# Hedgehog attention and a spatial gating unit on one core: another order of the same work

## The chip, the cores and the metric

The kernel runs on one core of a Trainium2 chip. A core has five engines that each work through their own queue of instructions: PE (TensorE, matrix products), DVE (VectorE), ACT (ScalarE), POOL (GpSimd) and SP (SyncE, which here only issues transfers). The metric is the time of one launch on the device in microseconds, the median over several runs.

## The reference

Two stages follow each other. The first is linear attention with a softmax-like feature map: every query and key vector of 64 numbers is projected to 128, the largest absolute value is taken off, and exponentials of both signs give 256 features. The second is a gated MLP whose gate mixes the 576 positions of a sequence.

```python
def phi(x):                                   # x is q or k: 8 batches, 8 heads, 576 positions, 64
    proj = einsum('bhsd,df->bhsf', x, w_phi)  # 128 features
    proj = proj - max(abs(proj), axis=-1, keepdims=True)
    return concatenate([exp(proj), exp(-proj)], axis=-1)
...
kv  = einsum('bhsf,bhsd->bhfd', k_p, v);  z = sum(k_p, axis=2)
num = einsum('bhsf,bhfd->bhsd', q_p, kv)
den = einsum('bhsf,bhf->bhs', q_p, z)[..., None] + 1e-06
x   = num / den                               # reshaped to 8 batches, 576 positions, 512
...
h = maximum(x @ w_in, 0.0)                    # 1024 wide
u, v = h[..., :512], h[..., 512:]
v_n = (v - mean(v)) / sqrt(var(v) + 1e-06)
v_s = einsum('ts,bsd->btd', w_spatial, v_n) + b_spatial[None, :, None]
out = (u * v_s) @ w_out
```

## The kernel before

Each batch of 576 positions is cut into 512, which are four chunks of 128, and a tail of 64. Two batches share one tail tile of 128 rows, and four such pairs are worked beside the eight batches. All products are in bfloat16, all sums in eight banks of 2 KB per partition.

The code has no loop over batches. Every step is a small function marked `@op`, and a string, `ORDER`, lists some 1,400 words, each of which calls one step. A word reads `name.arguments:places@engine`: `tkc.0.1.0@V` is the copy of transposed keys of batch 0 on VectorE (A is ScalarE, P GpSimd, S SyncE), and the places are the banks or the numbered buffers that it writes. The last lines of the kernel walk through the string. No scheduler changes the order: each engine gets its instructions as the words stand, and a wait holds back all that is queued behind it on that engine.

The steps of one batch, with the lines at which the profile shows them:

- `lk`, `lq` load keys and queries by GpSimd's transfer queue (lines 358 and 362), `lv`, `lkt` and others on SyncE's. For batch 0 the keys come in four quarters as 32-bit numbers (`lkf`), and `ckf` casts each (line 257). `lin`, `lout`, `lsp` load weights by GpSimd's queue.
- `tk`, `tq` transpose on TensorE (line 488), `tkc`, `tqc` copy the result into T (line 257 on VectorE, line 255 on ScalarE).
- `kp`, `qp` project (line 540). `km`, `qm` reduce to the largest absolute value into mk and mq: on VectorE, line 545.
- `ke` and `qe` take the exponentials on ScalarE (lines 549 and 675). For keys the factor of the maximum goes into the values: `kem`/`kee` (line 554), then `vs` on GpSimd (line 605; for tails `vst`, line 620). `kv` multiplies (lines 640 and 642), `kvc` copies.
- For queries the maximum is split (`qs`, lines 657 and 658), transposed (`qt`, line 662), copied into mT (`qc`), and taken off as a second product into the same bank (`qf`, lines 666 and 670).
- `qn` multiplies with kv (line 724), `qr` and `qx` divide (lines 730 and 737). `tx` transposes x, `txc` copies.
- `vm` and `um` are the two halves of the first layer (lines 839 and 937); `vr` and `ur` evict with a relu (line 261 on ScalarE, 263 on VectorE). `vb`, `va`, `vx`, `vy` are the statistics (lines 867, 873, 844 and 847), `vw` the root on GpSimd (line 850), `vn` the normalised values (line 853).
- `sm` mixes the positions (lines 952 and 954), `sg` gates (line 961), `om` is the last layer (line 966), `oc` copies it, `od` stores it.
- A further `t` in a name (`vrt`, `vnt`, `omt`) is the same step for a pair of tails.
- `omh`, `och`, `odh` do one tile of the last batch in two halves of 256 columns (lines 985 and 997), so that the last store is small.
- `warm` and `warmh` are fillers: matmuls of 512 or 256 columns (lines 334 and 342) on zeros, whose result no one reads.
- `cident`, `csel`, `csel2`, `cphi`, `zvnt`, `chalf` make constants; `spt`, `spc`, `spb` transpose the spatial weights into w_spT and put the bias row behind them. `spb` is four small casts on GpSimd.

Numbers behind a name count batch, chunk or half: `km.4.0` reduces the first quarter of the keys of batch 4.

Of the kernel before, what the change touches and what calls it, by code (L numbers as in the profile page):

```python
# [17 lines left out]
zsp@V lq0.4.4:0 zvst.0@V lq0.0.4 cident@P csel@V csel2@V lkf.0:0@A lkf.1:1@S lphi@A lkf.3:2@S zvnt.0@V ckf.0:1@V  # L18
lkt.0:0@S ckf.1@P cphi@V warm.10:0 tk.0.0.0:0 tk.0.0.1:1 zmhl.0@V tkc.0.0.0:0@V tkc.0.0.1@A warm.3:2 kp.0.0:2,3
kp.0.1:4,5 ke.0.0.0:0 lkf.2:3@S km.0.1:0 warm.4:6 tq.0.1.1:0 tqc.0.1.1:1@V tq.0.1.0:1 ke.0.0.1 lv.0.0:0@S tqc.0.1.0@V  # L20
ckf.3@P tk.0.1.1:6 tkc.0.1.1:2@A km.0.0 lqt.0:1@S kem.0.1:0 vsz.0.1:0@P ke.0.1.0:1 chalf@P warm.4:7 kp.0.3:0,1
km.0.3:1 zmhl.2@V lq.1:2 ckf.2@V ke.0.1.1 warm.3:7 tq.0.0.0:2 tq.0.0.1:3 qp.0.0.1:6,7 tqc.0.0.1:3@V ckt.0:0@P
warmh.2:2 tkt.0:4 lk.1:0 tqc.0.0.0@A ke.0.3.0:2 lin.0 tk.0.1.0:5 tktc.0:0@V tkc.0.1.0@V qp.0.0.0:2,3 vs.0.1.1@P
warm.1:4 kp.0.2:4,5 lq.2:1 lin.1 ke.0.3.1 qm.0.0.1:0 ke.0.2.0:3 qm.0.0.0 kpt.0:0,1 qp.0.1.0:6,7 qm.0.1.0:1 qs.0.0:0@P
qp.0.1.1:2,3 warm.1:6 qt.0.0:6 ket.0.0:0 vs.0.1.0@P kem.0.0 qm.0.1.1 ket.0.1 qc.0.0:0@A kmt.0:2 cqt.0:0@V warm.2:7
qf.0.0.0:6,7 ke.0.2.1 qf.0.0.1:2,3 km.0.2 warm.4:0 tq.1.0.1:0 tqc.1.0.1:4@V tqt.0:1 tqtc.0:0@V qs.0.1:2@P vsz.0.0:1@P
qt.0.1:4 qc.0.1:1@V qe.0.0.0.1:0 vs.0.0.0@P lvt.0:0@S tq.1.1.1:5 kemt.0:1 qe.0.0.0.0 tq.1.0.0:6 qe.0.0.1.0:1
tq.1.1.0:7 qpt.0:0,1 tqc.1.0.0@V tqc.1.1.1:5@V kem.0.2:2 vs.0.0.1@P qmt.0:2 vstz.0:0@P warm.2:4 qf.0.1.1:4,5
qe.0.0.1.1 qp.1.1.0:2,3 qm.1.1.0:3 lv.0.1:1@S vst.0.0.0@P vsz.0.2:2@P tqc.1.1.0@A vst.0.0.1@P kv.0.1:6 qp.1.0.1:0,1
qe.0.1.1.1:2 kv.0.0:7 qm.1.0.1:0 qe.0.1.1.0 kem.0.3 qp.1.1.1:2,3 qm.1.1.1 kvc.0.0:0@A qst.0:0@P kvc.0.1@A qf.0.1.0:4,5  # L30
lkt.1:0@S vs.0.2.1@P vs.0.2.0@P lbs:0@S tk.1.0.0:7 tk.1.0.1:0 qtt.0:1 qct.0:2@V qe.0.1.0.1:3 tkc.1.0.1:6@V qe.0.1.0.0
# [116 lines left out]
            qf=5, rc=3, x=3, xt=1, xT=3, xTt=2, vr=5, st=4, mv=6, rs=5, vn=3, vnt=2, uT=3, uTt=2, ob=5)  # L148
# [933 lines left out]
```

## Time and profile before

| what | us |
|---|---|
| median of 3 runs | 257.66 |
| lowest and highest | 256.53, 257.89 |
| profiled execution | 256.3 |
| its span, first instruction to last | 254.2 |
| TensorE busy | 244.1 (96%) |
| VectorE busy | 222.3 (87%) |
| ScalarE busy | 192.0 (76%) |
| GpSimd busy | 156.2 (61%) |

A row of instructions reads: line, engine, operation, what it writes and reads, shape and count, then busy time. The chain of waits is followed back from the last instruction: at each step to what released it, or to the instruction before it on its engine. A row of it gives start, length and what it was. A row of busy time by stretch gives for each engine the time and the count of instructions begun. PE's pieces overlap, since a matmul starts while the one ahead drains.

### The profile page before, as it was taken

To read this page: it belongs to the slowest core of one execution; us is meant where nothing else is said; L and a number is where in the kernel's file an instruction comes from. 1 tells how busy PE (TensorE), PEld (TensorE's weight loads), DVE (VectorE), ACT (ScalarE), POOL (GpSimd) and SP (SyncE) were. 2 spreads that over 40 slices of the span, in tenths; PEclk is the share of its full clock that TensorE was granted. 3 is DMA by queue.
4 is the path that set the end of the run, shared out by engine and by line. 5 is a ranking of instruction groups with operands and counts; after the bars stand their busy time and mean duration, and the time that the engine had idled before them with its cause. 6 is when DMAs were issued, how large, how long until landed. Compare 5 with 4: busy or idle time off the path is not lost.

```text
span 254.2 us, 8049 instructions
## 1 busy us (share of the span) xinstructions
PE 244.1 (96%) x3298; PEld 150.0 (59%) x3298; DVE 222.3 (87%) x417; ACT 192.0 (76%) x300; POOL 156.2 (61%) x244
## 2 busy tenths in 40 slices
PE   6968999999999999999999999999999999999994
PEld 2646865876546675756575555566566664545542
DVE  6899999999999999999999999899778883966472
ACT  2799999999999989969998986879997821122321
POOL 5399998829695879799879263675394130085000
PEclk9999999999999999999999999999999999999999
DMA  7999999899999499759989999194424606004265
GB/s 177 262 217 210 208 213 207 149 289 225 151 167 201 74 237 187 191 73 185 127 185 188 210 307 212 25 229 143 125 85 44 85 9 160 0 3 165 83 200 213
DMA packets 77911, 40.79 MB, mean 160 GB/s; under 512 B 46770, under 2 KB 73266, under 8 KB 77876
## 3 DMA queue, kind: packets, MB, share of 16 engines
q1 hardware_dynamic: 59956, 29.77, 54.3%
q0 software_dynamic: 17424, 10.10, 29.7%
q8 instruction: 25, 0.41, 0.7%
q10 hardware_dynamic: 496, 0.43, 0.5%
q14 instruction: 10, 0.08, 0.1%
HBM read 32.82 MB, written 9.44 MB: 166 GB/s over the span
## 4 chain that ended last, share of the span: by engine, by line
PE 63%; DVE 21%; POOL 7%; issue 6%; ACT 1%; DVEq 0%; POOLq 0%; ACTq 0%
PE banks L952 10%; PE banks L966 9%; PE banks L839 9%; PE banks L937 7%; DVE mk L545 6%; PE banks L640 5%; DVE mq L545 5%; PE banks L724 4%; PE banks L540 4%; POOL vs L605 3%; PE banks L954 2%; PE banks L666 2%; PE banks L670 2%; PE banks L1032 1%; DVE x L737 1%
## 5 line engine op out<-in xcount | busy, mean ns | idle before, releaser
L675 ACT ACTIVATE qf<-banks 128x1024 bf16<-128x1024 f32 x72 | 70.4, 1037 | 8.8 <-PE banks L670 6.4
L605 POOL TENSOR_TENSOR vs<-v,em 128x512 bf16<-128x512 f32 x62 | 64.0, 1048 | 6.3 <-ACT em L554 4.7
L549 ACT ACTIVATE kf<-banks 128x1024 bf16<-128x1024 f32 x64 | 63.0, 1038 | 3.1 <-PE banks L540 1.9
L545 DVE TENSOR_REDUCE mk<-banks 128x8 f32<-128x1024 f32 x36 | 43.3, 1212 | 0.8 <-PE banks L540 0.7
L545 DVE TENSOR_REDUCE mq<-banks 128x8 f32<-128x1024 f32 x36 | 43.1, 1216 | 0.6 <-PE banks L540 0.2
L850 POOL TENSOR_TENSOR rs<-mv,neghalf 128x4 f32<-128x4 f32 (+2 forms) x13 | 11.1, 855 | 45.0 <-DVE mv L844 44.8
L952 PE MATMUL banks<-w_spT,vn 128*128 128x512 bf16 x128 | 32.9, 379 | 0.1
L839 PE MATMUL banks<-w_v,xT 128*128 128x512 bf16 x128 | 32.6, 379 | 0.1
L937 PE MATMUL banks<-xT,w_u 128*128 128x512 bf16 x128 | 32.4, 379 | 0.1
L966 PE MATMUL banks<-w_out,uT 128*128 128x512 bf16 x124 | 30.7, 379 | 0.0
L255 ACT COPY ob<-banks 128x512 f32<-128x512 f32 (+1 forms) x21 | 12.3, 592 | 22.1 <-PE banks L966 21.7
L961 DVE TENSOR_TENSOR uT<-banks,uT 128x512 bf16<-128x512 f32 x32 | 21.4, 684 | 4.7 <-PE banks L954 3.9
L867 DVE BATCH_NORM_STATS2 st<-vr 128x6 f32<-128x512 bf16 x32 | 21.5, 678 | 4.0 <-ACT vr L261 3.9
L640 PE MATMUL banks<-vs,kf 128*128 128x66 bf16 x512 | 23.9, 194 | 0.1
L640 PEld LDWEIGHTS <-kf 128*128 128x128 bf16 x512 | 21.6, 97 | 3.7 <-issue 0.2
L540 PE MATMUL banks<-wphi,T 64*128 64x128 bf16 x512 | 22.8, 217 | 0.9 <-DVE mq L545 0.3
L261 ACT ACTIVATE vr<-banks 128x512 bf16<-128x512 f32 (+1 forms) x22 | 13.3, 611 | 12.3 <-POOL vn L853 5.9
L737 DVE TENSOR_TENSOR x<-banks,rc 128x512 bf16<-128x512 f32 x32 | 21.8, 686 | 0.8 <-DVE rc L730 0.2
L853 POOL TENSOR_SCALAR vn<-vr,mv,rs 128x512 bf16<-128x512 bf16 x27 | 20.4, 764 | 2.5 <-DVE mv L847 1.8
L724 PEld LDWEIGHTS <-qf 128*128 128x128 bf16 x512 | 19.1, 97 | 3.8 <-ACT qf L675 0.2
L642 PE MATMUL banks<-vst,kft 128*128 128x66 bf16 x128 | 21.1, 192 | 0.0
L540 PEld LDWEIGHTS <-T 64*128 64x128 bf16 x512 | 15.6, 94 | 8.9 <-issue 6.3
(122 smaller groups left out, 454.3 us busy)
## 6 DMA issues: line engine op xcount, KB each, us to landing
v<-in_v_dram SPq DMA_DIRECT2D x16, 512.0 KB, 9.2
out_dram<-ob SPq DMA_DIRECT2D x31, 256.0 KB, 2.6
ld<-in_q_dram POOLq DMA_DIRECT2D x7, 512.0 KB, 9.9
ld<-in_k_dram POOLq DMA_DIRECT2D x7, 512.0 KB, 9.0
out_dram<-ob SPq DMA_DIRECT2D x9, 128.0 KB, 2.5
tf<-in_k_dram SPq DMA_DIRECT2D x8, 128.0 KB, 7.4
tf<-in_q_dram SPq DMA_DIRECT2D x8, 128.0 KB, 7.8
vt<-in_v_dram SPq DMA_DIRECT2D x8, 128.0 KB, 5.2
```

The lines of the kernel that those rows point to most:

```text
L540: nc.tensor.matmul(out=bank(banks[y])[:, n * F:(n + 1) * F], lhsT=xT[halves[y], n, :], rhs=wphi[halves[y], :], start=True, stop=True)
L545: nc.vector.tensor_reduce(out=out_, in_=pp.rearrange("p y (n f) -> p y n f", f=F), axis=AX.X, op=ALU.max, apply_absolute_value=True)
L549: nc.scalar.activation(out=kf[:, s].rearrange("p y n f -> p y (n f)"), in_=pp, func=AF.Exp, bias=0.0, scale=(1.0, -1.0)[s])
L605: ENG[e].tensor_tensor(out=at["vs", (b, j)][:, s, :, 0:D], in0=at["v", (b, j // 2)][:, (j % 2) * n:(j % 2 + 1) * n, :], in1=at["em", (b, j ...
L640: nc.tensor.matmul(out=pv[:, hh, s, :], lhsT=kf[:, s, c % 2, 2 * hh + c // 2, :], rhs=w[:, s, NB * hh + c, :], start=(c == 0), stop=False)
L675: nc.scalar.activation(out=at["qf", u][:, s].rearrange("p y n t -> p y (n t)"), in_=at["pq", u], func=AF.Exp, bias=0.0, scale=(1.0, -1.0)[s])
L724: nc.tensor.matmul(out=at["pn", u][:, y, n, :], lhsT=f[:, s, y, n, :], rhs=at["kv", b][:, hg * HH + n, s, :], start=(s == 0), stop=(s == 1))
L737: nc.vector.tensor_tensor(out=at["x", (b, cc)][:, :, hg * HH:(hg + 1) * HH, :], in0=at["pn", u][:, :, :, 0:D], in1=at["rc", u].to_broadcas ...
L839: nc.tensor.matmul(out=bank(place)[r], lhsT=lhs[:, kc, r], rhs=w_v[:, kc, :], start=(kc == 0), stop=(kc == KC - 1))
L937: nc.tensor.matmul(out=bank(place).rearrange("p (c t) -> p c t", c=NB), lhsT=w_u[:, kc, dc * P:(dc + 1) * P], rhs=at["xT", b][:, :, kc, :] ...
L952: nc.tensor.matmul(out=bank(place), lhsT=at["vn", b][:, c, cs], rhs=w_spT[:, c, 0:T0], start=(c == 0), stop=False)
L966: nc.tensor.matmul(out=bank(place), lhsT=at["uT", b][:, dc, c * P:(c + 1) * P], rhs=w_out[:, dc, :], start=(dc == 0), stop=(dc == KC - 1))
```

## The change

Only the string `ORDER` is another one. The functions, the buffers and their numbers stay. Nearly every line of the string differs; what differs in substance:

- Fillers: 40 of 512 columns where there were 34, and the two of 256 columns (`warmh.2`) are gone. All stand in the first part of the table, ahead of batch 1's first layer.
- Engines of copies, with their number: `qc` five from ScalarE to VectorE and two back, `tkc` three from ScalarE to VectorE; `ur` six and three, `vr` six and four, `oc` five and eight (to ScalarE the second of each); `ckf.1` goes from GpSimd to VectorE, `ckf.2` from VectorE to GpSimd, two `vs` of batch 7 from VectorE to GpSimd.
- The order at the start, `spb` on GpSimd, loads on SyncE's and GpSimd's queues, and the order of the last tiles; the tile that is stored in halves is (7,2) instead of (7,1).

The last words of the table:

```diff
-om.7.3:2 oc.7.3:0@V od.5.3@S od.7.3@S om.7.0:3 om.7.2:0 oc.7.0:4@V od.7.0@S oc.7.2:2@A od.7.2@S omh.7.1.0:1
-omh.7.1.1:0 och.7.1.0:1@A odh.7.1.0@S och.7.1.1:3@V odh.7.1.1@A
+od.7.3@S od.7.1@S om.5.3:6 oc.5.3:2@A od.5.3@S omh.7.2.0:7 omh.7.2.1:0 och.7.2.0:1@A odh.7.2.0@S och.7.2.1:3@V
+odh.7.2.1@A
```

In the old words the second half output `omh.7.1.1` writes bank 0, which `om.7.2` wrote two products earlier. In the new ones `omh.7.2.1` writes bank 0, and the products ahead of it (`om.5.0:6 om.7.0:7 om.7.3:4 om.7.1:5 om.5.3:6`) use others.

VectorE's queue at the start of the program, before. `sel` is a constant for the queries' maxima, `vnt` a buffer that is preset, `ld` the keys, `T` their transposed copy:

```order
L301 TENSOR_TENSOR sel_169<-ident 128x16
L303 TENSOR_TENSOR sel_169<-sel_169 128x8
L307 TENSOR_SCALAR sel<-sel_169 128x1024
L257 COPY vnt_153<-ident 128x512 x2
L257 CAST ld_63<-ob_160 128x512
L257 CAST wphi<-wphi_f 64x128 x2
L316 MEMSET mhl_107 128x64
L257 COPY T_65<-banks 128x512
L545 TENSOR_REDUCE mk_87<-banks 128x2x4
```

The same place after the change:

```order
L301 TENSOR_TENSOR sel_169<-ident 128x16
L303 TENSOR_TENSOR sel_169<-sel_169 128x8
L257 COPY vnt_153<-ident 128x512 x2
L257 CAST ld_62<-ob_161 128x512
L257 CAST ld_62<-ob_160 128x512
L257 CAST wphi<-wphi_f 64x128 x2
L307 TENSOR_SCALAR sel<-sel_169 128x1024
L257 COPY T_65<-banks 128x512 x2
L316 MEMSET mhl_109 128x64
L545 TENSOR_REDUCE mk_87<-banks 128x2x4
```

A second cast of keys stands ahead of the first copy and the first reduction, `sel` is behind the weights' casts, and both copies of the first keys come ahead of the reduction.

GpSimd's queue between the values of batch 1 (`vs`) and the first normalised values of batch 0 (`vn`), before:

```order
L358 DMA ld_62<-in_k_dram 128x8x256
L422 DMA vn_150<-in_moe_w_spatial_dram 128x2304
L257 CAST w_spT<-uT_155 1x512
L257 CAST w_spT<-uT_155 1x64
L257 CAST w_spT<-uT_155 1x512
L257 CAST w_spT<-uT_155 1x64
L605 TENSOR_TENSOR vs_95<-v_74,em_94 128x8x64 x2
```

And after the change, where the four casts stand again:

```order
L605 TENSOR_TENSOR vs_98<-v_75,em_91 128x8x64 x2
L850 TENSOR_TENSOR rs_145<-mv_140,neghalf 128x4
L257 CAST w_spT<-uT_155 1x512
L257 CAST w_spT<-uT_155 1x64
L257 CAST w_spT<-uT_155 1x512
L257 CAST w_spT<-uT_155 1x64
L853 TENSOR_SCALAR vn_151<-vr_134,mv_140,rs_145 128x512
L853 TENSOR_SCALAR vn_151<-vr_130,mv_140,rs_145 128x512
L257 CAST tl_76<-tf_78 128x512
L362 DMA ld_64<-in_q_dram 128x8x256
```

`spb` has moved from ahead of batch 1's `vs` to between the root of batch 0 (`vw.0.2`) and the first `vn`, and two loads that stood ahead of that root now come behind.

ScalarE's last instructions, before:

```order
L261 ACTIVATE uT_2_157<-banks_61 128x512
L255 COPY ob_3_163<-banks_61 128x512
L255 COPY ob_2_162<-banks_61 128x512
L255 COPY ob_1_161<-banks_61 128x256
L997 DMA out_0_dram<-ob_3_163 128x256
```

And after the change:

```order
L255 COPY ob_3_163<-banks_61 128x512
L255 COPY ob_4_164<-banks_61 128x512
L255 COPY ob_0_160<-banks_61 128x512
L255 COPY ob_2_162<-banks_61 128x512
L255 COPY ob_1_161<-banks_61 128x256
L997 DMA out_0_dram<-ob_3_163 128x256
```

Four full output copies in a row now stand on ScalarE ahead of the half one, where there were two.

More of the change, by code (lines that the diff above doesn't have):

```diff
@@ L17 @@
 ORDER = """
[L18 to L31, printed above, removed]
-kv.0.2:6 tkc.1.0.0@A vs.0.3.0:3@P qn.0.0.0:2,3 qft.0:0,1 kvc.0.2@V qr.0.0.0:0 qx.0.0.0:0 qet.0.0:4 vsz.0.3@P
```

233 lines of the change are left out of this document (124 added, 109 removed).

## The prediction

> **What bounds the kernel now.** I read the page's totals and its chain first, then busy time by stretch, then the long pieces of the chain in order of time, and last the start, the middle and the tail piece by piece.
>
> ```profile
> span 254.2 us, 8049 instructions
> PE 244.1 (96%) x3298; PEld 150.0 (59%) x3298; DVE 222.3 (87%) x417; ACT 192.0 (76%) x300; POOL 156.2 (61%) x244
> ...
> PE 63%; DVE 21%; POOL 7%; issue 6%; ACT 1%; DVEq 0%; POOLq 0%; ACTq 0%
> ```
>
> TensorE holds 63% of the chain and VectorE (DVE) 21%. An average hides where each rules, so next the busy time of every engine by stretch:
>
> ```profile
> core 0: us, PE busy (x) PEld busy (x) DVE busy (x) ACT busy (x) POOL busy (x), PEclk, DMA share, GB/s
> ...
> 12.00:20.00 8.00, 5.64 (x88) 3.60 (x87) 7.91 (x12) 7.57 (x13) 7.54 (x13) 1.00 1.30 213
> ...
> 50.00:75.00 25.00, 24.93 (x313) 15.28 (x310) 24.49 (x48) 24.16 (x38) 16.76 (x29) 1.00 1.35 216
> 75.00:100.00 25.00, 24.43 (x416) 16.59 (x416) 24.71 (x47) 23.36 (x35) 18.85 (x30) 1.00 0.99 170
> ...
> 220.00:245.00 25.00, 25.00 (x152) 11.91 (x150) 16.73 (x36) 6.06 (x11) 9.33 (x12) 1.00 0.31 106
> ```
>
> From 12 us to 100 us VectorE is busy almost without a hole (7.91 of 8.00; 24.71 of 25.00). TensorE seems as full after 50 us, but pipelined matmuls overlap in that column, so a short stall doesn't show there. At 220 us only TensorE is full (VectorE 16.73 of 25.00). So there are two regimes. First VectorE's back-to-back queue sets when TensorE may go on; later TensorE's own work does. The chain shows the border:
>
> ```profile
> 6.20 0.62 PE banks L488 x8
> 6.82 0.65 PE banks L334 x3
> 7.46 0.60 PE banks L540 x16
> ...
> 30.58 0.94 ACT qf L675
> ...
> 91.72 0.68 DVE x L737
> ...
> 97.04 1.73 PE banks L839 x8
> ...
> 103.44 0.97 PE banks L952 x4
> ...
> 107.26 0.51 PE banks L724 x16
> ...
> 119.51 1.15 DVE mq L545
> 120.66 1.01 DVE mk L545
> ...
> 198.88 0.97 PE banks L952 x4
> ```
>
> After 91.72 the chain is TensorE's except for a return to VectorE at 119.51. Eight 512-column matmuls without a wait take 1.73, so four take 0.86; groups of four that show about 0.97 hold a small stall of 0.11 each, and there are eleven such from the one at 103.44 to the one at 198.88.
>
> In the first regime time is set by the **lag**: VectorE's work ahead of an instruction minus TensorE's work ahead of the matmul that needs it. If a table raises it by 1 us at the worst place, the end moves by 1 us; less VectorE work that doesn't lower it there is worth nothing.
>
> **The change part by part.** The instructions are the same but for the fillers and the engine of some copies, so each part is a move. The sum is made against the profiled execution, 256.3 us (span 254.2 and 2.1 around it); it lies 1.36 below the median of the runs, 257.66, and I carry the same difference over.
>
> *Start.* These rows tell how VectorE comes to its first reduction:
>
> ```profile
> 1.51 3.84 PE L334 MATMUL banks<-w_spT 128*128 128x512 bf16 x10 [1.51 <-DVE w_spT L329]
> ...
> 3.99 0.69 DVE L307 TENSOR_SCALAR sel<-sel 128x1024 bf16<-128x1024 bf16 x1
> 4.60 1.20 DVE L257 COPY vnt<-ident 128x512 bf16<-128x512 bf16 x2
> 5.72 0.42 DVE L257 CAST ld<-ob 128x512 bf16<-128x512 f32 x1
> ...
> 7.00 0.36 DVE L257 COPY T<-banks 128x512 bf16<-128x512 bf16 x1
> 8.09 1.23 DVE L545 TENSOR_REDUCE mk<-banks 128x8 f32<-128x1024 f32 x1 [0.72 <-PE banks L540]
> ```
>
> The key cast ckf.1 joins VectorE ahead of the first reduction and the 0.69 of `sel` moves behind the weights' cast, so the first copy of T comes some 0.55 later (7.55 for 7.00) and the reduction at 8.64. In return ckf.2 (0.42) leaves VectorE for GpSimd (POOL), the identity is made before the query's two DMA issues, and two copies change places. Added up along the queue, both tables end the reductions of the first query half near 18.3. Cost 0; the ends are −0.3 (a better fit of the copies) and +0.55 (none of it made up).
>
> *Fillers.* Six more full fillers and two half ones fewer are a net of five full ones. Three fillers in a row take 0.65 in the chain (6.82), which is 0.216 each: 5 × 0.216 = 1.08 us of TensorE time, all before 40 us. There TensorE has 2.36 us free in the eight from 12 us on, waiting on VectorE. So they cost 0, and up to 1.08 where that cover is gone.
>
> *Engines.* By count up to the same VectorE instruction. The prices:
>
> ```profile
> L257 DVE COPY T<-banks 128x512 bf16<-128x512 bf16 x18 | 7.1, 410 | 0.1
> ...
> L257 DVE CAST kv<-banks 128x264 bf16<-128x264 f32 x15 | 6.4, 425 | 0.3 <-PE banks L642 0.2
> ...
> L263 DVE TENSOR_SCALAR vr<-banks 128x512 bf16<-128x512 f32 x14 | 9.4, 676 | 2.0 <-POOL vn L853 1.9
> ...
> L257 DVE COPY mT<-banks 128x128 bf16<-128x128 bf16 x12 | 2.5, 211 | 0.0
> ...
> L257 DVE COPY ob<-banks 128x512 f32<-128x512 f32 x15 | 10.2, 684 | 4.4 <-PE banks L966 4.3
> ```
>
> - Up to km.4.0, the first key reduction of batch 4 (near 97 us in the trace): VectorE has three T copies and two mT copies more, two other copies of T's size, two of kv and a vr fewer: 1.23 + 0.42 − 0.82 − 0.85 − 0.68 = −0.70. TensorE has one vm (0.86) and one kv group (20 matmuls of 66 columns; 16 take 0.51, so 0.64) fewer: −1.5. Lag +0.8.
> - Up to qx.3.1.1, the division at 91.72 where the chain leaves VectorE: VectorE −1.1 (three T copies, two mT more; three of T's size, an ob copy, a statistic and small ones fewer), TensorE one om and one vmt fewer, −1.72. Lag +0.6.
> - Up to km.5.1, the reduction that the chain has at 120.66: VectorE about +0.9, TensorE one om, kv group and um more, +2.4. Lag −1.5.
>
> So the place that ends the first regime comes 0.6 us later, and the return to VectorE at 119.51 has 1.5 us more room. I take **+0.6** for the first (ends 0 and +0.8), since 91.72 is the row at which the chain changes hands. For the second, what there is to win is about 0.4 at 119.51 to 129 and the eleven groups at 0.11, 1.2: at most 1.6. I take a third, **−0.5** (ends 0 and −1.6), as a group of 0.97 may just as well stand in the new order.
>
> *spb on GpSimd.* The four casts of the bias row move from ahead of batch 1's vs to behind vw.0.2, straight ahead of batch 0's vn:
>
> ```profile
> 35.95 2.60 POOL L257 CAST w_spT<-uT 1x512 bf16<-1x512 f32 x4
> ...
> 39.78 3.04 POOL L605 TENSOR_TENSOR vs<-v,em 128x512 bf16<-128x512 f32 x3 [1.23 <-issue]
> ...
> 54.45 0.16 DVE L844 TENSOR_SCALAR mv<-mv 128x4 f32<-128x4 f32 x1
> ...
> 57.51 1.05 POOL L850 TENSOR_TENSOR rs<-mv,neghalf 128x4 f32<-128x4 f32 x1
> ...
> 58.67 1.52 POOL L853 TENSOR_SCALAR vn<-vr,mv,rs 128x512 bf16<-128x512 bf16 x2
> ...
> 60.67 0.70 DVE L263 TENSOR_SCALAR vr<-banks 64x512 bf16<-64x512 f32 x1 [0.15 <-POOL mhl L658]
> ...
> 69.97 1.04 PE L952 MATMUL banks<-w_spT,vn 128*128 128x512 bf16 x4
> ```
>
> At the old place 1.23 us of idle followed, so the 2.60 were free. At the new one, vw waits for mv, which VectorE gives 1.1 us later in the new order: 55.7. The root takes 1.05, spb 2.60, the first vn 0.76: done at 60.2. VectorE's eviction vrt.0.1, which needs that vn's source buffer, stands at 60.7 in its queue. It is hidden with half a microsecond to spare: cost 0, ends 0 and +2.1 (below). Late next would be the other vn, at 60.9 to 65.0, and vnt at 68.4; the spatial matmuls need all five from 69.97 on. The loads moved on the queues of SP and GpSimd (lq.4 and lk.4 some 10 us later, lv and xk earlier) land more than 6 us ahead of their first reader by the same count: cost 0, and a stall of a transfer shorter than that costs nothing either.
>
> *Tail.*
>
> ```profile
> 249.34 0.60 PE L985 MATMUL banks<-w_out,uT 128*128 128x256 bf16 x4
> 249.58 0.86 ACT L255 COPY ob<-banks 128x512 f32<-128x512 f32 x2 [2.05 <-PE banks L966]
> 250.22 0.60 PE L985 MATMUL banks<-w_out,uT 128*128 128x256 bf16 x4 [0.28 <-ACT ob L255]
> ```
>
> The second half output now writes bank 0, which ScalarE (ACT) is still emptying of om.7.2: the group starts 0.88 after the first, where the first half's matmuls take 0.43 (half of 0.86). In the new table bank 0 has long been read. The wait goes: **−0.44** (ends 0 and −0.44); late next is only the last copy and its DMA, as before.
>
> Sum: 0 + 0 + 0.6 − 0.5 + 0 − 0.44 = −0.34, so 255.96 profiled and **257.3** as a median.
>
> *A rule weighed.* The ten fillers at 1.51 start 0.43 apart, three later ones take 0.65 together, 0.22 each; PEclk reads 1.00 in both. The Trainium skill, "TensorE: Matmul & The Clock Gate", section "Part 1: The HAM clock gate (the "warmup" mystery)", has the array at half rate until about 3.4 us of sustained work, and again after an idle window of that length; the two spacings agree with it. By that rule more early fillers make a half-rate start less likely, and the sum stays as it is unless the release comes late.
>
> **The rivals.**
> - *B, faster: the relief of ScalarE counts.* Three T copies and a net of two mT copies leave it, and the chain's only long ScalarE piece (0.94 at 30.58) stands behind them. Then the middle gives −0.94 in place of +0.6, the late stalls go whole (−1.6), the tail −0.44: −2.98, **254.7**. For it: ScalarE is busy 24.16 of 25 from 50 us on. Against: VectorE is no less full there, and what left ScalarE went to it.
> - *C, slower: spb takes the place of the wait.* If vw.0.2 starts later than 56.2 against VectorE's 60.7 (the point from which it decides), VectorE stands idle at vrt.0.1 for vn, in its full stretch, and all behind it is late. Price up to 2.60 less the 0.5 of room, 2.1, on top of the +0.6, with −0.44 at the tail and no late gain: +2.26, **259.9**. For it: in the trace VectorE came to this very eviction with 0.15 idle, just behind vn, so there is no reserve, and POOL is 7% of the chain. Against: the walk above.
> - *S: the start isn't made up.* +0.55 at the first reduction and +0.8 of lag, −0.44: +0.9, **258.6**.
> - *D: the half rate lasts past the ten fillers.* The matmuls needed first (8 transposes at 6.20 and 16 projections at 7.46, 0.62 + 0.60 in the chain) would take as long again, +1.22 on the sum of −0.34: **258.5**. Against: PEclk 1.00 and the 0.22 spacing right after.
>
> That the table does nothing measurable is within the forecast.
>
> **How the numbers follow.** Half a per cent is 1.3 us, about what a measurement here can tell: faster means below 256.4, slower above 258.9. Forecast 0.40 (its own range 256.0 to 258.6, split 0.12 faster, 0.22 same, 0.06 slower), B 0.22, C 0.24, S 0.10 (0.06 same, 0.04 slower), D 0.04 (half and half). That makes faster 0.34, same 0.30, slower 0.36. The range reaches to B with −0.3 at the start and to C with +0.55: 254.2 to 260.5.
>
> **What would show it.** Start: the first mk reduction at about 8.6, and the first query half's last one done at 18.3 again. Fillers: idle of TensorE before 40 us down by a microsecond, nothing else. Middle: the chain leaves VectorE near 92.3; spb at 57 to 59.5 and VectorE without idle at the first vrt on line 263 that follows. Late: fewer groups of 0.97 between 100 and 200, none on VectorE at 120. Tail: the two L985 groups 0.43 apart. I'm wrong if VectorE shows a hole behind vn at 60 us, if its busy share from 12 to 100 us falls, or if TensorE waits for GpSimd or for a transfer.

## The result, and the profile after

| | median, us | against before, 95% |
|---|---|---|
| before (11 runs beside after) | 256.74 | |
| after (11 runs) | 258.28 | 1.0053 [1.0032, 1.0074] |
| after, measured again (12 runs) | 258.17 | 1.0040 [1.0021, 1.0059] |

The change makes the kernel slower: by 1.0 to 1.4 us by the ratios, which are ratios of means, and by 1.3 to 1.5 us by the medians (before has 256.88 beside the second measurement). The forecast was 257.3; the time lies in its range, but moved the other way than the sum of −0.34. The profiled execution of after took 258.28 too, with a span of 256.5; that of before, 256.3, was 0.44 below the median of the runs beside after, so a difference of the two profiles shows about half a microsecond too much.

The page of after, totals and shares of its chain of waits:

```profile
span 256.5 us, 8090 instructions
PE 245.3 (96%) x3302; PEld 149.4 (58%) x3302; DVE 220.0 (86%) x419; ACT 191.1 (74%) x294; POOL 159.2 (62%) x248
...
PE 83%; DVE 5%; POOL 4%; DMA 3%; issue 2%; ACT 1%; ACTq 0%; SPq 0%; POOLq 0%
```

VectorE has 2.3 us less work and its share of the chain falls from 21% to 5%, and still the end is later. That the chain is made of TensorE now doesn't mean that TensorE's useful work sets the end: fillers are TensorE too. Busy time by stretch:

```profile
12.00:20.00 8.00, 6.98 (x82) 3.51 (x79) 7.94 (x12) 7.99 (x13) 7.35 (x13) 1.00 1.30 214
...
50.00:75.00 25.00, 23.87 (x331) 15.40 (x329) 24.54 (x46) 23.72 (x39) 17.14 (x28) 1.00 1.14 178
75.00:100.00 25.00, 24.81 (x420) 16.39 (x418) 24.51 (x45) 24.41 (x36) 21.32 (x32) 1.00 0.90 160
```

From 12 to 20 us TensorE is busy 6.98 where it was 5.64, and VectorE has no more in it than before (7.94 for 7.91). From 50 to 75 us TensorE has 1.06 less. Instruction by instruction, traces of kernels with the same order show that VectorE's queue moves as a whole in the first 100 us: once it is late by some amount, it stays so. Two things that make it late are tried below: the fillers up to 40 us and one instruction at 56 us. At 104 us (`km.4.3`) VectorE is 1.15 later than before. The last matmul, near 251, ends 0.49 later. From its end to the end of the span after then takes 5.20 us, where before takes 3.40. So of the 2.29 us between the two spans, 1.80 lie behind the last matmul.

### The profile page after: what moved, and what is told of

Its sections match the earlier page's. It is cut to its first block, busy times and chain, and to the rows that moved or that the text cites. A ratio compares the mean times of both kernels' runs of the same rounds, so it can differ in the third digit from the quotient of the medians.

```text
span 256.5 us, 8090 instructions
## 1 busy us (share of the span) xinstructions
PE 245.3 (96%) x3302; PEld 149.4 (58%) x3302; DVE 220.0 (86%) x419; ACT 191.1 (74%) x294; POOL 159.2 (62%) x248
## 4 chain that ended last, share of the span: by engine, by line
PE 83%; DVE 5%; POOL 4%; DMA 3%; issue 2%; ACT 1%; ACTq 0%; SPq 0%; POOLq 0%
PE banks L839 13%; PE banks L952 11%; PE banks L937 11%; PE banks L966 9%; PE banks L540 7%; PE banks L640 6%; PE banks L724 6%; PE banks L666 3%; PE banks L670 3%; PE banks L954 3%; DMA wphi_f<-in_w_phi_dram 2%; PE banks L642 2%; DVE x L737 2%; PE banks L488 1%; PE banks L1004 1%
## 5 line engine op out<-in xcount | busy, mean ns | idle before, releaser
L605 POOL TENSOR_TENSOR vs<-v,em 128x512 bf16<-128x512 f32 x64 | 65.8, 1045 | 8.6 <-ACT em L554 7.0
L545 DVE TENSOR_REDUCE mq<-banks 128x8 f32<-128x1024 f32 x36 | 43.4, 1214 | 1.3 <-PE banks L540 1.0
L545 DVE TENSOR_REDUCE mk<-banks 128x8 f32<-128x1024 f32 x36 | 43.4, 1214 | 0.8 <-PE banks L540 0.6
L850 POOL TENSOR_TENSOR rs<-mv,neghalf 128x4 f32<-128x4 f32 (+2 forms) x13 | 11.0, 845 | 32.5 <-DVE mv L909 15.8
L255 ACT COPY ob<-banks 128x512 f32<-128x512 f32 (+1 forms) x25 | 14.4, 588 | 17.7 <-PE banks L966 11.9
L853 POOL TENSOR_SCALAR vn<-vr,mv,rs 128x512 bf16<-128x512 bf16 x27 | 20.6, 768 | 8.6 <-DVE mv L847 8.1
L540 PE MATMUL banks<-wphi,T 64*128 64x128 bf16 x512 | 23.0, 217 | 1.4 <-DVE T L257 0.7
L540 PEld LDWEIGHTS <-T 64*128 64x128 bf16 x512 | 15.6, 94 | 10.7 <-issue 7.2
L261 ACT ACTIVATE uT<-banks 128x512 bf16<-128x512 f32 x19 | 11.5, 607 | 13.7 <-PE banks L937 12.6
L724 PE MATMUL banks<-kv,qf 128*128 128x66 bf16 x512 | 20.6, 193 | 0.7 <-issue 0.5
## 6 DMA issues: line engine op xcount, KB each, us to landing
out_dram<-ob SPq DMA_DIRECT2D x31, 256.0 KB, 2.8
```

The source lines that it names most:

```text
L540: nc.tensor.matmul(out=bank(banks[y])[:, n * F:(n + 1) * F], lhsT=xT[halves[y], n, :], rhs=wphi[halves[y], :], start=True, stop=True)
L545: nc.vector.tensor_reduce(out=out_, in_=pp.rearrange("p y (n f) -> p y n f", f=F), axis=AX.X, op=ALU.max, apply_absolute_value=True)
L605: ENG[e].tensor_tensor(out=at["vs", (b, j)][:, s, :, 0:D], in0=at["v", (b, j // 2)][:, (j % 2) * n:(j % 2 + 1) * n, :], in1=at["em", (b, j ...
L724: nc.tensor.matmul(out=at["pn", u][:, y, n, :], lhsT=f[:, s, y, n, :], rhs=at["kv", b][:, hg * HH + n, s, :], start=(s == 0), stop=(s == 1))
```

## The experiments

Each kernel is compared with runs of before on the same chip. The ratios are ratios of means, so they differ a little from what the medians give. All kernels:

| kernel | median | ratio to before, 95% |
|---|---|---|
| e1 before, with the tail of after | 257.62 | 1.0021 [0.9995, 1.0048] |
| e2 after, with the tail of before | 258.30 | 1.0051 [1.0031, 1.0072] |
| e3 after, with the start of before | 267.56 | 1.0372 [1.0319, 1.0425] |
| e4 before, with the start of after | 257.67 | 1.0033 [1.0009, 1.0058] |
| e5 after, `ckf.2` on VectorE | 257.65 | 1.0028 [1.0013, 1.0043] |
| e6 after, 34 fillers for 40 | 257.79 | 1.0031 [1.0011, 1.0052] |
| e7 before, with after's first 653 words | 259.13 | 1.0085 [1.0050, 1.0121] |
| e8 after, with before's first 137 words | 258.27 | 1.0056 [1.0034, 1.0077] |
| e9 after, spb ahead of the root | 257.46 | 1.0007 [0.9989, 1.0025] |
| e12 after, spb behind the first vn | 257.51 | 1.0017 [1.0002, 1.0031] |
| e11 after, a sixth output buffer | 258.04 | 1.0039 [1.0027, 1.0052] |
| e10 after, e5, e6, e9 and e11 together | 257.50 | 1.0020 [1.0002, 1.0038] |
| e13 after, stores spread | 258.30 | 1.0047 [1.0025, 1.0069] |
| e14 after, e13, e9 and e6 together | 257.05 | 1.0003 [0.9983, 1.0023] |
| e16 before, 21 fillers for 34 | 256.46 | 0.9976 [0.9961, 0.9991] |
| e17 after, spb as in e9, 23 fillers | 256.22 | 0.9977 [0.9958, 0.9996] |
| e18 before, the first ten fillers alone | 258.36 | 1.0030 [1.0009, 1.0052] |

### Which part of the table: start, middle or tail

Six kernels are put together from the two tables, cut at a word and continued with the other's words; a word that would be missing or doubled is put in or left out at the seam, and banks and buffers are renamed to fit.

e1, the tail alone. Before up to the issue of `odt.3`, then the tail of after:

```diff
 sg.7.3 odt.3@S
-om.5.3:0 oc.5.3:3@A sg.7.2 om.7.3:2 oc.7.3:0@V od.5.3@S od.7.3@S om.7.0:3
+sg.7.2 om.7.0:7 om.7.3:0 oc.7.0:3@A om.7.1:1 oc.7.3:4@A od.7.0@S oc.7.1:0@A
...
```

> The table before up to its last product of batch 5 and the gate of (7,2); from there the last output tiles, their stores and the half tile in the order of the changed table. Theory A, the loss sits in the stores of the tail (the last half copy waits for a store that still reads its buffer, and four full stores bunch ahead of the last ones): +1.0 to +1.6 us over before, with the last half copy about 0.9 us behind the last matmul instead of 0.4. Theory B, the loss sits in the first 36 us: the tail alone gains what the forecast gave it, -0.44 us, and at most 0.2 is lost.

e2, all but the tail. After up to `sm.7.2`, then the tail of before:

```diff
 od.5.2@S sm.7.2:5
-sg.7.2 om.5.0:6 om.7.0:7 oc.5.0:1@V om.7.3:4 od.5.0@S oc.7.0:3@A om.7.1:5
+om.5.0:6 oc.5.0:1@V od.5.0@S om.5.3:4 oc.5.3:3@A sg.7.2 om.7.3:0 oc.7.3:0@V
...
```

> The changed table up to the same place, and from there the last tiles as before. Theory A: 1.0 to 1.6 us less than the changed kernel, so within 0.6 us of before. Theory B: 0.4 us more than the changed kernel, since the wait on bank 0 comes back, so about 2 us over before.

Measured: e1 is 0.54 above before with an interval that holds zero and reaches to 1.2, and e2 is as slow as after. Neither theory's number came. The tail of before doesn't mend after: in e2's trace the last matmul ends 0.71 later than in after, and what follows it is 0.80 shorter. By these two times the tail alone isn't the whole loss; how large its share is they leave open.

e3 and e4, the start (to about 38 us) alone:

```diff
 lv.1.0:2@S txc.0.0@V km.1.0 kp.1.3:4,5
-tq.2.1.1:0 qt.1.1:7 vmt.0.0:6 lqt.1:1@S
+lqt.1:1@S qt.1.0:1 qc.1.0:1@V lv.1.1:3@S kp.1.2:0,1
...
```

> The table before up to the first relu of batch 0 (some 36 us), then the changed table. Theory B, GpSimd's queue is late in the first 25 us (the cast ckf.2 and the two weight loads stand ahead of the values) and VectorE never makes it up: 0.7 us less than the changed kernel, +0.8 over before. Theory A alone: no change against the changed kernel, +1.5 over before.

```diff
 vr.0.2:0@A zmhl.0@V km.1.0
-kp.1.2:0,1 ke.1.3.1:0 vm.0.1:7 tkt.1:6
+lq.3:1 vst.0.1.1@P qs.1.1:2@P vst.0.1.0@P tq.2.1.1:0 qt.1.1:7 vmt.0.0:6
...
```

> The changed table up to the same place at some 36 us, then the table before. Theory B: +0.7 us over before, as VectorE is 0.7 us late there and is the bound until 92 us. Rival: what VectorE is late at 36 us is made up in the waits that the table before holds later, and the time is that of before within 0.2 us.

e3 came out at 267.56. Its trace has a stall of TensorE of 4.27 us, for which the profile names no releaser:

```profile
59.05 0.21 PE L722 MATMUL banks<-kv,qf 128*128 128x66 bf16 x1 [4.27 <-issue]
```

(In e1 to e4 line numbers are two or three lower than elsewhere.) The loads of keys and queries go round three buffers, and a load of keys that is issued at 47.04 lands at 60.02, near the end of the stall. That the seam makes this load late, and the load the stall, is argued and not shown. Either way e3 says nothing of the start. e4 loses 0.33%, but in its trace too part of the loss lies behind the seam: GpSimd waits for a buffer before it can issue a load of queries, the root behind it is late, and VectorE's `vrt.0.1` then stands waiting for the first vn:

```profile
62.87 0.69 DVE L260 TENSOR_SCALAR vr<-banks 64x512 bf16<-64x512 f32 x1 [1.09 <-POOL vn L850]
```

This is the wait that rival C was built on, but in after itself it doesn't occur. What e4 does show: by this place VectorE was 2.19 late, and every later instruction up to 192 us was late by the same 2.19. So in the order of before a lateness of VectorE's queue in the first 100 us goes to the end undiminished. A gain need not: e17 below is 1.18 ahead of after at 64 us and only 0.58 from 126 us on, since at 121 us VectorE waits for TensorE.

e7 and e8 move the seam to about 103 us and to 23 us.

```diff
 kv.3.2:0 kvc.3.2@A kvc.3.3@V
+qs.4.1:2@P xk.5.1:5@S cqt.2:0@P lkt.3:0@S smt.0.1:7 od.0.1@S
...
```

> The changed table up to the last key exponential of batch 4 (some 106 us), then the table before to the end. If the loss is made in the first regime (theory B): VectorE is 1.1 to 1.5 us late at the cut and stays so, +1.0 to +1.5 us over before. If it is made in the second half or the tail: +0.4 us or less.

```diff
 qe.0.1.1.1:2 kv.0.0:7 qm.1.0.1:0 qe.0.1.1.0 kem.0.3
+qst.0:0@P lkt.1:0@S vsz.0.3:3@P vs.0.2.0@P kvc.0.0:0@A qp.1.1.1:0,1
...
```

> The table before up to the projections of batch 1's queries (some 25 us; its fillers, casts and loads with it), then the changed table. Theory B: 0.5 to 0.7 us less than the changed kernel, with the first kv group at 24.1 us. Rival, the loss is made later, in the order between 25 and 60 us: the time of the changed kernel within 0.2 us.

e7 lost more than after does. Its profiled execution took 263.87 us against a median of 259.13, so its trace is read only up to the seam, where its VectorE is as late as in after. That is no verdict on the second half. e8 gained nothing, with 0.9 us lost in the trace at its seam. Both are misses: cutting tables that are this closely interlocked makes a third table.

### spb

Single instructions of after's trace tell more. Around spb, GpSimd and VectorE of after:

```profile
54.80 1.04 POOL L850 TENSOR_TENSOR rs<-mv,neghalf 128x4 f32<-128x4 f32 x1 [5.94 <-DMA T<-ld]
55.91 2.60 POOL L257 CAST w_spT<-uT 1x512 bf16<-1x512 f32 x4
...
56.04 0.99 DVE L847 TENSOR_SCALAR mv<-mv 128x4 f32<-128x4 f32 x1
56.95 1.21 DVE L545 TENSOR_REDUCE mk<-banks 128x8 f32<-128x1024 f32 x1
```

L847 works on four columns. Of its eight instructions of this shape in after, five take 0.16 or 0.17, and two take 0.39 and 0.34, both while GpSimd works. Here it takes 0.99, and ends when the first of spb's casts (1.09 of the 2.60) does. It waits for no semaphore. Two experiments move spb alone:

```diff
 vs.1.3.1@P
+spb@P
...
-vw.0.2:0@P kmt.1:2 spb@P
+vw.0.2:0@P kmt.1:2
```

> After, with spb put back ahead of the root of batch 0, where GpSimd has nothing to do from 48.9 to 54.8 us. Theory: where the changed table has it, spb's first cast (1.09 us on one partition) holds VectorE's L847 of four columns for its length, 0.99 where the others take 0.16; that 0.85 is carried to the end. Then L847 near 56 takes 0.16, the trace is 0.85 earlier from 57 us on, and the median is 257.4 to 257.5. Rival 1, spb was hidden (the prediction's cost 0): L847's 0.99 has another cause and stays, 258.3. Rival 2, it stays hidden further on (the lost time is made up by TensorE before 100 us): earlier at 57, but not at 100 us, 258.3.

```diff
-spb@P kp.2.0:2,3 qm.2.0.1 km.2.0:1 vn.0.3:1@P
+kp.2.0:2,3 qm.2.0.1 km.2.0:1 vn.0.3:1@P spb@P
```

> After, with spb one place later, behind the first vn of batch 0. GpSimd is as late with the second vn and the loads as in the changed table; only the moment of the casts is another, 0.76 later, when VectorE has no instruction of four columns. Theory (VectorE is held by the cast): L847 takes 0.16, the median is 257.4 to 257.5, as with spb ahead of the root. Rival (GpSimd's lateness is what costs): no gain, 258.3, while the kernel with spb ahead of the root gains.

e9, GpSimd and then VectorE:

```profile
48.94 2.67 POOL L257 CAST w_spT<-uT 1x512 bf16<-1x512 f32 x4
...
56.05 0.16 DVE L847 TENSOR_SCALAR mv<-mv 128x4 f32<-128x4 f32 x1
56.12 1.22 DVE L545 TENSOR_REDUCE mk<-banks 128x8 f32<-128x1024 f32 x1
```

e12:

```profile
57.30 2.61 POOL L257 CAST w_spT<-uT 1x512 bf16<-1x512 f32 x4
...
56.09 0.16 DVE L847 TENSOR_SCALAR mv<-mv 128x4 f32<-128x4 f32 x1
56.16 1.22 DVE L545 TENSOR_REDUCE mk<-banks 128x8 f32<-128x1024 f32 x1
```

In both L847 is back at 0.16 and the reduction behind it comes 0.83 and 0.79 earlier; both gain 0.7 in the median against after measured again (258.17), though on another chip and with intervals that still overlap its interval. e12 holds the rest fixed: GpSimd is later still with its second vn (59.90 for 59.27 in after), so its lateness isn't what cost. The cost was that spb's cast ran at the moment of a small VectorE instruction. Not every small one is held: in e9 a form of L847 of 64x1 took 0.13 at 49.20, under the first of the moved casts. The Trainium skill, "Trainium Architecture — The Big Picture", section "What this means for kernel authors", says that VectorE and GpSimd share a pair of ports which is held as an exclusive lock, not divided. The rows agree with a lock; that it is this one they can't show. Of the 0.83, a wait for TensorE takes 0.36 back two microseconds later, and part of that is won again; from 65 us on the shift is 0.63.

### The cast and the fillers at the start

e5 takes the cast of the third quarter of the first keys back to VectorE:

```diff
-lq.1:2 lqt.0:1@S km.0.3:1 tq.0.0.0:3
+lq.1:2 lqt.0:1@S km.0.3:1 ckf.2@V tq.0.0.0:3
...
-qm.0.0.1:0 ckf.2@P tktc.0:0@V
+qm.0.0.1:0 tktc.0:0@V
```

> The changed kernel with one word put back: the cast ckf.2 on VectorE behind the fourth key reduction, as before, in place of GpSimd. Theory B1, the cast's 0.6 us on GpSimd is what makes the tail values and with them the first kv group late (24.85 us): that group starts at about 24.3, VectorE is some 0.5 us less late at 36 us, and the time falls by 0.5 us. Rival: VectorE pays the 0.35 us itself and nothing is won: the time of the changed kernel within 0.2 us.

The median is 0.5 to 0.6 lower than after's, but the intervals overlap, and in the trace VectorE is 0.19 ahead of after at 80 us, 0.17 of it from an earlier first load. I take the cast's move as undecided, and small.

e6 takes six full fillers out:

```diff
-warm.3:5
+warm.2:5
...
-warm.4:1 qf.0.0.0:4,5 warm.5:1
+warm.3:1 qf.0.0.0:4,5 warm.3:1
...
-warm.2:3
+warm.1:3
...
-km.1.1:3 warm.1:4 kp.1.0:4,5
+km.1.1:3 kp.1.0:4,5
```

> The changed kernel with 34 full fillers in place of 40 (one each out of four places, two out of one). Theory F, the fillers stand in the way: 1.0 to 1.3 us less than the changed kernel. Theory B and the prediction: they lie in waits, and the time stays within 0.2 us.

TensorE around two of these groups (L334) in after:

```profile
17.57 1.03 PE L334 MATMUL banks<-w_spT 128*128 128x512 bf16 x4
18.53 0.39 PE L666 MATMUL banks<-T,wphi 64*128 64x512 bf16 x2
...
19.08 1.25 PE L334 MATMUL banks<-w_spT 128*128 128x512 bf16 x5
20.17 0.39 PE L516 MATMUL banks<-ident,tl 128*128 128x128 bf16 x4
```

and in e6:

```profile
17.16 0.81 PE L334 MATMUL banks<-w_spT 128*128 128x512 bf16 x3
18.16 0.39 PE L666 MATMUL banks<-T,wphi 64*128 64x512 bf16 x2 [0.19 <-DVE mq L545]
...
18.71 0.82 PE L334 MATMUL banks<-w_spT 128*128 128x512 bf16 x3
19.81 0.40 PE L516 MATMUL banks<-ident,tl 128*128 128x128 bf16 x4 [0.28 <-DVE tl L257]
```

In after no useful matmul waits: it starts right behind the last filler, so its input was there already, and TensorE was the late one. In e6 there is a wait of 0.19 and 0.28 for VectorE, which is how a filler should end: before its input comes. Of after's eleven filler groups behind the first ten fillers, ten end without such a wait. The median falls by 0.4 (overlapping intervals); the trace is clearer. One reduction of batch 3's keys (L545), the same in all four, at about 80 us, in after, e6, e9 and e14:

```profile
80.60 1.21 DVE L545 TENSOR_REDUCE mk<-banks 128x8 f32<-128x1024 f32 x1
...
79.91 1.20 DVE L545 TENSOR_REDUCE mk<-banks 128x8 f32<-128x1024 f32 x1
...
79.97 1.21 DVE L545 TENSOR_REDUCE mk<-banks 128x8 f32<-128x1024 f32 x1
...
79.47 1.21 DVE L545 TENSOR_REDUCE mk<-banks 128x8 f32<-128x1024 f32 x1
```

e6 is 0.69 ahead of after, e9 0.63, and both edits together (e14) 1.13. Their first reductions near 8.5 were ahead by 0.23, 0.07 and 0.13, from the first load. That leaves 0.46 for the fillers, 0.56 for spb and 1.00 for both: they add up. The 0.46 come in small steps: 0.09 at 16 us, 0.11 by 26, 0.19 at 38 and 0.07 at 54. A caution goes with them: the second execution of after differs from the first by 0.5 between 28 and 32 us, on a wait for TensorE (L724), with the very same instructions. So the size for the fillers, read off one pair of executions, is less sure than that for spb, which lies at one instruction.

### The tail

Issue and landing of the full output stores (L977) from 240 us on, first before, then after (duration of the issue min/median/max, first and last start; then from issue to landing):

```profile
L977 SPq DMA_DIRECT2D out_dram<-ob x7: 332/333/529, 240.8 to 250.2; - x7
DMA to landing us min/median/max: 2.3/2.4/2.7
...
L977 SPq DMA_DIRECT2D out_dram<-ob x7: 332/392/1253, 243.9 to 251.1; - x7
DMA to landing us min/median/max: 2.7/3.3/3.4
```

Seven stores go out in 7.2 us where it was 9.4, and take 0.9 longer to land. The last copy of before, then the last pieces of after:

```profile
250.91 0.42 DVE L257 COPY ob<-banks 128x256 f32<-128x256 f32 x1 [1.54 <-PE banks L985]
...
250.26 1.04 PE L985 MATMUL banks<-w_out,uT 128*128 128x256 bf16 x8
...
252.01 0.42 DVE L257 COPY ob<-banks 128x256 f32<-128x256 f32 x1 [4.25 <-DMA out_dram<-ob]
```

Both half groups run through without the bank's wait, as forecast. But the last copy, into buffer 3, waits for the store of (7,0) from the same buffer. From the last matmul to the end of the span it is 3.40 us in before, and the same in e16 and e18, which share its last words; it is 5.20 and 5.08 in the two executions of after, and 4.5 to 5.3 in e5, e6, e9, e12 and e17, which share after's.

e11 gives the last copy a sixth buffer:

```diff
-uTt=2, ob=5)
+uTt=2, ob=6)
...
-och.7.2.1:3@V
+och.7.2.1:5@V
```

> After, with a sixth buffer for output tiles, in which the last half copy goes; nothing else. Theory: the last copy, at 252.01, waited 0.61 for the store of (7,0) to free its buffer; with a buffer of its own it starts at about 251.4, the last store is issued 0.6 earlier, and the median is 257.7. Rival: the stores share the queues and land no earlier (they take 2.7 to 3.4 us here against 2.3 to 2.4 before), so that an earlier issue takes as much longer: 258.3.

In its trace the copy waits for TensorE alone and starts 0.86 earlier (0.19 of it because TensorE's last matmul ends earlier), but the end comes only 0.48 earlier:

```profile
251.15 0.42 DVE L257 COPY ob<-banks 128x256 f32<-128x256 f32 x1 [3.58 <-PE banks L985]
```

In the median it is 0.13 to 0.24 below after: nearer the rival, the stores land hardly earlier, and 4.90 are left behind the last matmul. From 251 to 254 us the DMA engines are full in after (shares of 1.09, 1.06 and 1.07; before has 0.50 and 0.00 from 252 on). e13 therefore moves two products ahead, between the mixing products of batch 7, so that their stores go out sooner; it has the sixth buffer too:

```diff
-om.5.2:5 sm.7.0:4 sm.7.3:6 sg.7.3 oc.5.2:2@A sg.7.0 od.5.2@S sm.7.2:5
-sg.7.2 om.5.0:6 om.7.0:7 oc.5.0:1@V om.7.3:4 od.5.0@S oc.7.0:3@A om.7.1:5
+om.5.2:5 sm.7.0:4 om.5.0:2 sm.7.3:6 om.5.3:3 sg.7.3 oc.5.2:2@A oc.5.0:1@A oc.5.3:5@A sg.7.0
+od.5.2@S od.5.0@S od.5.3@S sm.7.2:5 sg.7.2 om.7.0:7 om.7.3:4 oc.7.0:3@A om.7.1:5
...
```

> After, with two of the five output products that stand at its end, om.5.0 and om.5.3, moved ahead between the mixing products of batch 7, so that their stores fall into 244 to 248 us, where the 16 DMA engines are busy 0.29 of 246 to 248; a sixth output buffer for one of them, all else as in after. Theory: after's tail is set by the stores that queue up: from the last matmul to the end it has 5.2 us against 3.4 of before, and the DMA engines are full from 250 to 254. With the stores spread the tail takes 3.4 to 3.9 from the last matmul, and the median is 257.0 to 257.4. Rival: the tail's length comes from the last copy and its store alone (the kernel with a sixth buffer gained 0.24), or the moved products let TensorE run dry behind the mixing of (7,2): 258.0 or more.

The stores land sooner (2.3 in the median), but now TensorE stands waiting for `sg.7.3`, whose cover these products were:

```profile
248.46 2.33 PE L966 MATMUL banks<-w_out,uT 128*128 128x512 bf16 x10 [0.35 <-DVE uT L961]
```

In the trace the last matmul ends 0.37 later than in after, and 4.23 us follow it instead of 5.20: the transfers gain more than TensorE loses. But that execution (257.67) is the fastest of the twelve, and the median is after's (258.30 against 258.17). Why the gain doesn't show in it stays open. No edit of the tail alone gave a gain in the median that can be told from zero, while in the traces the stretch behind the last matmul is the largest part of the difference from before. The two don't fit together, and no run here settles it.

### Together

e10 has the edits of e5, e6, e9 and e11 in one:

> After with all four repairs: spb ahead of the root, the cast ckf.2 on VectorE, 34 full fillers for 40, a sixth output buffer. By the sums of the single steps, -0.85 - 0.65 - 0.55 - 0.6, it would be 255.6, 1.2 below before, and the late gain of the new order (0.5 to 0.7 between 100 and 250 us) would show. If the repairs of the start overlap (cast and fillers relieve the same wait), 256.2. Rival: the first regime isn't what sets the end any more after the first 0.7, and TensorE's own work does: 257.3 or more.

e14 is e13 ("the same" in what follows) with the edits of e9 and e6:

> The same, and spb ahead of the root, and 34 full fillers for 40. By the single results (0.8 for spb, 0.5 for the fillers, 1.0 for the spread stores) from 258.28: 256.0, 0.9 below before; if the fillers' part overlaps with spb's, 256.4. Rival: what is won in the first regime is lost behind it, as in the kernel with all four repairs (257.5): no better than the kernel with spread stores alone.

e15 is after, measured again:

> After, unchanged, as a yardstick on the same chip as the two kernels beside it: 258.0 to 258.5, its last matmul at about 251 and its end 5 us later. Both theories expect the same; if it is below 257.6 here, the gains of the other two are to be read against that.

e10 is no better than e9 alone (257.50 for 257.46): the sums didn't come. Its trace had a late load of queries near 9 us, which takes 0.55 away at the second key reduction:

```profile
9.48 0.84 PE L488 MATMUL banks<-ident,ld 128*128 128x128 bf16 x12 [0.37 <-DMA ld<-in_q_dram]
```

That is one execution, and e17 below has the same 0.55 in its trace; whether the cast on VectorE, which e14 lacks, is what keeps the median up stays open. e14 missed its own forecast of 256.0 to 256.4 too. But it reaches 257.05, 1.1 below after on the same chip and 1.25 below e13, from which it differs by spb and six fillers alone. Its interval and e13's lie apart. With these two mended the new order is level with before (1.0003). It gets there by another way: in e14's trace the last matmul ends 0.12 ahead of before's, and the stretch behind it is still longer (5.58 for 3.40; this execution, 258.05, is the slowest of its twelve).

### How many fillers

If fillers hold TensorE in after, they may do so in before. e16 takes 13 full ones and the two half ones out of before, e18 all behind the first ten, e17 takes 17 out of after and has spb where e9 has it:

```diff
-warm.10:0 ... warm.3:2 ... warm.4:6 ... warm.4:7 ... warm.3:7 ... warmh.2:2 ... warm.1:4 ... warm.1:6 ... warm.2:7 ... warm.4:0 ... warm.2:4
+warm.10:0 ... warm.2:2 ... warm.2:6 ... warm.2:7 ... warm.1:7 ... warm.1:7 ... warm.2:0 ... warm.1:4
```

> Before, with 21 full fillers where it has 34 and two half ones: the ten at the start stay, of the others about half go. In its trace nearly every filler group ends 0.21 to 0.34 us ahead of a useful matmul's start, the pace of a matmul behind another, so that matmul was ready and stood behind the filler. Theory (fillers hold what the start waits for): VectorE's queue is 0.3 to 0.8 earlier by 55 us, carried to the end, and the median is 0.3 to 0.8 below before. Rival (the prediction's: TensorE waits for VectorE there and the fillers cost nothing): equal to before within 0.2. Second rival: without them TensorE's clock or its waits get worse: slower.

```diff
-warm.10:0 ... warm.4:2 ... warm.4:6 ... warm.2:7 ... warm.1:5 ... warm.3:5 ... warm.2:4 ... warm.2:4 ... warm.4:1 ... warm.5:1 ... warm.2:3 ... warm.1:4
+warm.10:0 ... warm.2:2 ... warm.2:6 ... warm.1:7 ... warm.1:5 ... warm.1:4 ... warm.1:4 ... warm.2:1 ... warm.2:1 ... warm.1:3
```

> After, with spb ahead of the root and 23 full fillers for 40, the tail as in after. By the single steps (0.8 for spb, 0.5 for the first six fillers, 0 to 0.5 for eleven more): 256.4 to 256.9, at or below before. Rival: only the first six fillers cost, 256.9 to 257.1, as in the kernel with spread stores, spb and 34 fillers.

```diff
-warm.3:2 ... warm.4:6 ... warm.4:7 ... warm.3:7 ... warmh.2:2 ... warm.1:4 ... warm.1:6 ... warm.2:7 ... warm.4:0 ... warm.2:4
```

> Before, with the ten fillers at the start alone. Theory: more of the same, 0.5 to 1.0 below before, if nothing needs the fillers; where TensorE's granted clock or the spacing of its matmuls shows a loss from 6 to 35 us, slower than the kernel with 21. Rival (fillers cost nothing): equal to before.

e16 and e17 are faster than before, by 0.24% and 0.23%, with intervals that end just below 1, and are the two best kernels here. e18 is slower. Its stretches from 6 us on show why (the third number from the right is the granted clock):

```profile
6.00:12.00 6.00, 3.40 (x49) 2.63 (x49) 4.87 (x10) 4.43 (x8) 1.40 (x5) 0.88 1.26 271
12.00:20.00 8.00, 6.52 (x77) 4.49 (x77) 7.56 (x11) 7.42 (x12) 7.04 (x13) 0.50 1.31 215
```

Without fillers the clock falls to half (0.62 still from 20 to 30 us), and VectorE's queue is 2.3 late by 26 us. In e16 it falls too, but for 3.4 us only:

```profile
18.00:20.00 2.00, 2.00 (x21) 1.16 (x21) 2.00 (x3) 1.80 (x3) 1.79 (x5) 0.50 1.25 238
20.00:22.00 2.00, 2.00 (x19) 1.50 (x18) 2.00 (x4) 2.00 (x6) 1.86 (x5) 0.67 1.35 187
```

and still wins; e17 keeps 1.00 throughout:

```profile
6.00:12.00 6.00, 3.66 (x57) 2.18 (x56) 5.01 (x11) 3.62 (x7) 0.83 (x2) 1.00 1.24 244
12.00:20.00 8.00, 5.54 (x73) 3.17 (x74) 8.00 (x12) 8.00 (x14) 7.51 (x13) 1.00 1.35 196
```

So by the medians fillers aren't free in before either, and by e18 they aren't useless: there is a number between. Where e16's 0.6 us come from the traces don't show. Its VectorE is 0.13 later than in before at 55 us, and its span is 254.4 for 254.2. The trace of before, though, is one of its faster executions (256.3, with a median of 257.06 beside e16), so the two traces aren't fit to show it. That the fillers' hold on TensorE is the cause in before is argued, not shown.

## Why the prediction was wrong, point by point

- **Fillers, "So they cost 0".** This step failed. The 2.36 us that TensorE had free from 12 to 20 us were a sum over a stretch; a filler is paid for where it stands, if the matmul behind it is ready. In after ten groups of eleven had a ready matmul behind them, and six fillers fewer moved VectorE's queue by some 0.46 (in one pair of executions; the medians, 0.4 to 0.5, have intervals that overlap). Only 0.09 of it came between 12 and 20 us: the cover was read there, but fillers stand as late as 35 us, and from 20 to 50 us TensorE was busy 28.99 of 30 in before. The start of the useful matmul behind each group could have told, and in before too nearly all of them started without a wait. One of the prediction's signs of being wrong did show: from 12 to 100 us VectorE is busy 85.80 us where it was 86.51, and the 0.99 of L847 is counted as busy in that.
- **spb, "cost 0".** This failed as well. The walk was right in its direction (the root came at 54.80, earlier than the 55.7 forecast, and no wait for vn arose). But it asked only who waits for spb's result, not what spb's casts do to an instruction that runs beside them. Rival C had the place, a larger size (2.1 at most, 0.6 to 0.8 measured) and the wrong mechanism.
- **Engines, "+0.6".** The count was put to the wrong instruction. The figures, −1.1 on VectorE and −1.72 on TensorE, belong to the division `qx.3.1.1`, which the trace of before has at 115.88. The division at 91.72, where the chain changes hands, is `qx.2.1.1`; counted up to it VectorE has +0.56 and TensorE +0.44, a lag of 0.1. In e9, without spb's cost, it comes 0.33 after before's, less than the 0.46 that the fillers are put at, and in e14, without either, 0.16 ahead of before's: no lag was seen. The term should have been 0 to +0.1.
- **Late, "−0.5".** The size is about right. No VectorE piece is left in after's chain between 100 and 200 us, where before had a run of them from 119.51 to 129, and 0.66 of the 1.15 of lateness at 104 us are gone at the last matmul. But the groups of four at 0.97 were misread. They haven't become fewer: there are 16 from the one at 100.18 to the one at 190.79. And they hold no stall: TensorE has no idle time before any of their matmuls in either trace. In each trace all but one stand right behind a group of short matmuls (mostly projections, L540); these start 0.05 apart or less, but in after the first matmul of 512 columns starts 0.13 to 0.15 behind the last of them. So the 0.11 looks like the price of that neighbour, and not like a wait that another order ends.
- **Tail, "−0.44".** The wait for the bank is gone, as said. "Late next is only the last copy and its DMA, as before" failed: the copy waited for a buffer, and stores that come closer land later. By e1 the tail is worth +0.54, with an interval that holds zero. In the two profiled executions the stretch from the last matmul to the end is 1.80 longer than before, the largest single difference from the sum; the other kernels with after's last words and body have at least 4.5 there. So this step failed too, and by how much in the median stays open.
- **Start, "Cost 0".** The first reduction at 8.56 (8.6 forecast) and the end of the first query half near 18.4 (18.3) were right. So rival S, whose 258.6 came nearest to the time, did so by luck: the start was made up, and the 0.8 of lag that it adds wasn't there. What the cast on GpSimd costs is undecided.
- **The sum.** With spb and the fillers mended, the new order is +0.1 of before (e14) where the sum had −0.34 without them; the two terms put at zero were worth 1.1 to 1.25. That the time fell inside the range was the range's width, which reached to rivals with other mechanisms; its lower end, 254.2, is 0.2 below what its parts give (254.7 − 0.3).

Rival B, the relief of ScalarE, had no sign in any run. Rival D didn't occur: the clock reads 1.00 in after from the start.

## What to carry to other kernels

A filler should end before its successor's input arrives: look at each useful matmul behind a filler, and where none waits, the filler may be too long; where the clock stays at half, as in e18, there are too few. When an instruction moves on GpSimd, look also at which short VectorE instructions run at that moment. In a queue that has no slack, a loss of 0.5 us at 20 us is still a loss of 0.5 us at 100 us, however much room the totals of another engine show. And compare what follows the last matmul in both traces: here the stores went out closer together, landed later, and the stretch grew.

## What the runs showed of the hardware that was not expected

- A VectorE instruction of 128x4 numbers took 0.99 for 0.16 while a GpSimd cast on a single partition ran, and ended with it. A second, shorter case in after:

```profile
93.65 0.39 DVE L847 TENSOR_SCALAR mv<-mv 128x4 f32<-128x4 f32 x1
...
93.41 0.61 POOL L257 CAST tl<-tf 128x512 bf16<-128x512 f32 x1
```

  Under GpSimd's root (L850) and vn (L853) the same VectorE lines kept 0.14 to 0.16 in after, so not every GpSimd instruction does it; and forms of 64x1 (L847 in e9, L844 in after) kept 0.13 and 0.15 under casts, so not every VectorE instruction is held.
- The clock fell to 0.50 in e18 at 10.5 us, with no pause of TensorE longer than 1.35 us (the one that it fell in, from 9.3 us on), and in e16 at 17.9 us with none above 0.8 us ahead of it since 6.6 us. The Trainium skill, "TensorE: Matmul & The Clock Gate", section "Part 1: The HAM clock gate (the "warmup" mystery)", on which the prediction drew, has the clock fall after an idle window of about 3.4 us. Here shorter pauses were enough, so the measurement decides. The share of busy time in the 4 us ahead doesn't tell either: it was 1.61 us in e16 and 2.41 in e18, where the clock fell, and 2.41 in e17 over the same 6.5 to 10.5 us, 2.13 in e17 a little later and 2.01 in before (14.4 to 18.4), where it stayed. In e18 it came back only at 27.6 us, though TensorE was busy 3.91 of the 4 us from 12 to 16. What decides stays open.
- The issue of one store (7,0) took 1.25 us in after, 1.14 in its second measurement and 1.44 in e9, for 0.33 in e17, with nothing in the profile that it waits for. Why was not tried.
